# A memory-augmented recurrent attention layer: streamed weights, B-token keys and chain buffers rearranged

## The chip, the cores and the metric

The kernel runs on one core of one Trainium2 chip. The metric is the device time of one execution in microseconds (us); of several runs the median is taken. The engines are called as the profile calls them: PE (matmul), PEld (its weight load), ACT (scalar), DVE (vector), POOL (GpSimd), SP (SyncE, which here only issues transfers).

## What is computed

The model applies four layers to x of shape [1, 2048, 640]: A, B, A, B, each behind a layer norm and with a residual sum. Only A matters here. It cuts the 2048 rows into 64 segments of 32 and carries a memory of 8 rows from each segment to the next:

```python
# A, per segment s: xs = 32 normalised rows, mem = 8 rows
h = concatenate([mem, xs])                                   # L = 40 rows of 640
q, k, v = (einsum('td,dhe->hte', h, w) for w in (Wq, Wk, Wv))  # 32 heads of 192
mask = (idx[:, None] < M) | (idx[:, None] >= idx[None, :])   # M = 8
p = softmax(where(mask, einsum('hqe,hke->hqk', q, k) * 192 ** -0.5, -1e9))
o = einsum('hte,hed->td', einsum('hqk,hke->hqe', p, v), Wo)
mem = o[:8]                                                  # for the next segment
out[s] = o[8:]
```

The chain over segments is serial: the next segment's q, k and v of the memory rows need the memory rows of this one. Wq, Wk, Wv and Wo have 640 x 6144 elements each, in bf16 (6144 = 32 heads of 192). Layer B is a linear attention over all rows without such a chain.

## The kernel before

**Split of the tokens.** The last 8 of a segment's 40 tokens (the "B tokens") have K, Q and V that come from x alone, and their outputs do not enter the memory, so layer A runs in three parts. `A_pre` (L297 to L361) computes K, Q and V of the B tokens of all segments in large matmuls and stores them to DRAM (`kqb_d`, L350; `vb_d`, L361). `A_chain` (L363) walks the 64 segments with the 32 other tokens (8 of memory, 24 of x). `A_post` (L499) multiplies the B tokens' attention outputs with Wo.

**Rounds.** A segment is done in four rounds r of eight heads. In a round, three groups of 20 matmuls (L419, one group for each of K, Q, V) make the projections from hT, the transposed 32 tokens, and five k-blocks b of weights; the four PE row/column groups g of 32 work side by side. ACT evacuates K and Q to `raw` (L427), DVE transposes `raw` into QT (L429) and KT (L434 to L436); ACT and DVE copy V into Vp (L422, L424). The B tokens' Q is copied into QT by POOL (L409). Scores go into one PSUM bank: a mask by a matmul with an identity (L440), the keys of the 32 tokens (L445) and the keys of the B tokens (L449, 8 columns of kqb a head). ACT takes the exponent E (L453), PE sums it with a block of ones (L454, L456), ACT makes the reciprocal by lns and rc (L459, L461), DVE multiplies (Pt, L463 and L465). The values give O (L470; the B tokens' from vb, 8 rows, L474), which ACT and DVE copy into OT (L479, L480); POOL copies the B tokens' columns into otb (L481), and 48 matmuls add the round into W (L484).

**End of a segment.** DVE transposes the next rows (Hx) into hT (L383), transposes W into wt (L491), adds the residual Xr into ob (L494) and copies the new memory into hT (L492), with which the next segment begins. POOL stores otb (L487) and the four pieces of ob (L496).

**Weights.** A weight matrix is cut into 20 pieces (4 rounds, 5 k-blocks) of 128 x 1536 elements, 384 KB; there are 60 for K, Q and V. 36 stay in SBUF (b of 0 to 2, names wK, wQ, wV), 24 are streamed again in every segment: `pieces` (L284) loads b = 3 and 4 of one matrix and round together, 768 KB with rows of 6 KB, into a ring of three buffers called `wring` (L286), from copies that the kernel made at its start. That is 9.44 MB a segment. wo_res, all of Wo, is resident too.

**Order.** The program is written as loops, and a scheduler orders each engine's instructions; buffer counts of the pools decide how far ahead a load or a copy can go. SP issues the weights' ring, Xr (L377 to L379, from x or the residual) and Hx; POOL issues kqb (two a segment, L401), vb (eight a segment, L404), otb and ob. Xr, Hx, KT and Vp have two named buffers each; QT, E, lns, rc, Pt, OT, ob, kqb and vb two each from the pool.

Of the kernel before, what the change touches and what calls it, by code (L numbers as in the profile page):

```python
# [8 lines left out]
P = 128  # L9
BF16 = mybir.dt.bfloat16  # L10
# [5 lines left out]
MASK_NEG = -30000.0  # L16
LN_EPS = 1e-5
# [81 lines left out]
class Kernel:  # L99
# [73 lines left out]
    def build_B_consts(self, dram):  # L173
# [6 lines left out]
        with tc.tile_pool(name="bconst_tmp", bufs=1) as tp:  # L180
# [4 lines left out]
            dq = RR([nc.sync, nc.gpsimd])  # L185
# [14 lines left out]
    def layernorm(self, x_dram, xn_dram, li):  # L200
# [3 lines left out]
        with tc.tile_pool(name=f"ln{li}", bufs=3) as lp:  # L204
            dq = RR([nc.sync, nc.gpsimd])
# [24 lines left out]
    def build_A_consts(self):  # L230
# [3 lines left out]
        mk = const.tile([P, 112], BF16, name="mask_st")  # L234
        nc.gpsimd.memset(mk[:], 0.0)
        for e in range(2):
            m = mk[0:32, 40 * e + 16:40 * e + 40]
            nc.gpsimd.affine_select(out=m, in_=m, compare_op=ALU.is_ge, fill=MASK_NEG, base=8, pattern=[[1, 24]],
                                    channel_multiplier=-1)
            m = mk[0:32, 80 + 16 * e:80 + 16 * e + 8]  # L240
            nc.gpsimd.affine_select(out=m, in_=m, compare_op=ALU.is_ge, fill=MASK_NEG, base=0, pattern=[[1, 8]],
                                    channel_multiplier=-1)
            m = mk[0:32, 80 + 16 * e + 8:80 + 16 * e + 16]
            nc.gpsimd.affine_select(out=m, in_=m, compare_op=ALU.is_ge, fill=MASK_NEG, base=7, pattern=[[0, 8]],
                                    channel_multiplier=-1)
# [10 lines left out]
        for r in range(4):  # L256
            for m in "KQV":
                t = self.dram.tile([P, 2, 1536], BF16, name=f"wst{m}{r}")
                nc.sync.dma_start(out=t[:], in_=self.wview[m][:, 3:5, 1536 * r:1536 * r + 1536])
                self.wst[m, r] = t  # L260

    def layer_A(self, x_dram, xn_dram, xout_dram, li):
# [3 lines left out]
        NR = 4  # L266
        PW = 1536
        self.kqb_d = dram.tile([NSEG, P, NR, 224], BF16, name=f"kqb{li}")
        self.vb_d = dram.tile([NSEG * 8, NR, 4, 512], BF16, name=f"vb{li}")
        self.otb_d = dram.tile([NSEG, P, 384], BF16, name=f"otb{li}")  # L270
        wview = self.wview
        streamed = {(m, r, b) for m in "KQV" for r in range(NR) for b in (3, 4)}
        with tc.tile_pool(name=f"A{li}_wres", bufs=1) as wres:
# [10 lines left out]
            def pieces(pool, m, r, nb=3):  # L284
                t = pool.tile([P, 2, PW], BF16, name="wring", tag="wring", bufs=nb)
                nc.sync.dma_start(out=t[:], in_=self.wst[m, r][:])  # L286
                out = [res[m, r, b][:, :] for b in range(3)] + [t[:, 0, :], t[:, 1, :]]
                return out

            self.A_pre(xn_dram, li, pieces)  # L290
            for r in range(NR):
                nc.sync.dma_start(out=wo[:, 12 * r:12 * r + 12, :], in_=self.A_Wo.rearrange("h d m -> (h d) m").rearrange(
                    "(c p) m -> p c m", p=P)[:, 12 * r:12 * r + 12, :])
            self.A_chain(x_dram, xn_dram, xout_dram, li, pieces, wo)
            self.A_post(x_dram, xout_dram, li, wo)

    def A_pre(self, xn_dram, li, pieces):  # L297
# [4 lines left out]
        with tc.tile_pool(name=f"A{li}_pre", bufs=1) as pp, \  # L302
                tc.tile_pool(name=f"A{li}_preps", bufs=8, space=bass.MemoryType.PSUM) as ps_:
            xv = xn_dram.rearrange("(s t) d -> t s d", t=32)
            xBT = pp.tile([P, KC, 8 * NSEG], BF16, name="xBT")
            for k in range(NT):
                xb = pp.tile([P, 640], BF16, name="xB", tag="xB", bufs=1)
                for t2 in range(TP):
                    nc.gpsimd.dma_start(out=xb[NSEG * t2:NSEG * t2 + NSEG, :], in_=xv[24 + TP * k + t2])
# [4 lines left out]
                for t2 in range(TP):  # L314
                    t = TP * k + t2
                    ev.copy(out=xBT[:, :, :].rearrange("p b (s t) -> p b s t", t=8)[:, :, :, t],
                            in_=pt[:, 0:640].rearrange("p (b q) -> p b q", b=KC)[:, :, NSEG * t2:NSEG * t2 + NSEG])
            stage = [pp.tile([P, 16, 224], BF16, name=f"stage{i}") for i in range(2)]
            vst = [pp.tile([P, 4, 512], BF16, name=f"vst{i}") for i in range(1)]
            for t in stage:  # L320
                nc.vector.memset(t[:], 0.0)
            for t in vst:
                nc.vector.memset(t[:], 0.0)
# [410 lines left out]
```

## Time and profile before

| what | value |
|---|---|
| four runs | 5946.53, 5938.78, 5925.62, 5921.52 us, median 5932.2 |
| the profiled execution's own time | 5946.53 us |
| its span in the profile | 5944.4 us (2.1 us lie around it) |
| granted PE clock, mean | 0.877 |
| bytes moved | 1479 MB, mean 249 GB/s |
| ring loads | 1560 of 768 KB |
| chain, layer 1 | about 373 to 2540 us of the span |
| chain, layer 2 | about 3284 to 5500 us |
| A_pre of layer 1 | matmuls from 156 to 358 us |

How to read the profile: each engine has a share of busy time; 40 slices give busy tenths over the span and the bytes that the DMA engines moved. The chain that ended last follows the work back from the last instruction, so its shares say on what the end depended. A row of the timeline has start, length, engine, line, operation, result and operands, and how many were merged. Groups and waits name who ended an idle time; "issue" is time in which an engine waited for nothing that the profile shows. SPq, ACTq and POOLq are the engines' own issuing of transfers.

### The profile page before, as it was taken

To read this page: it belongs to the slowest core of one execution; us is meant where nothing else is said; L and a number is where in the kernel's file an instruction comes from. 1 tells how busy PE (TensorE), PEld (TensorE's weight loads), DVE (VectorE), ACT (ScalarE), POOL (GpSimd) and SP (SyncE) were. 2 spreads that over 40 slices of the span, in tenths; PEclk is the share of its full clock that TensorE was granted. 3 is DMA by queue.
4 is the path that set the end of the run, shared out by engine and by line. 5 is a ranking of instruction groups with operands and counts; after the bars stand their busy time and mean duration, and the time that the engine had idled before them with its cause. 6 is when DMAs were issued, how large, how long until landed. Compare 5 with 4: busy or idle time off the path is not lost.

```text
span 5944.4 us, 224613 instructions
## 1 busy us (share of the span) xinstructions
PE 4271.4 (72%) x99784; PEld 2569.8 (43%) x99784; DVE 2232.8 (38%) x6994; ACT 1587.3 (27%) x4729; POOL 1530.7 (26%) x3332
## 2 busy tenths in 40 slices
PE   0877777777777777757858677777777777777778
PEld 0744444444444444434337344444444444444343
DVE  2333333333333333337454333333333333332383
ACT  0322222222222222223123222222222222222230
POOL 3122233233333323220011332233333222332100
PEclk9988888888888988879879888888898888888888
DMA  5668888888888888840066788888888888887201
GB/s 186 234 223 295 299 297 306 286 305 301 301 304 297 306 297 296 295 136 1 21 222 209 270 300 299 297 299 303 294 311 303 289 292 287 298 309 240 92 22 32
DMA packets 423998, 1479.35 MB, mean 249 GB/s; under 512 B 119392, under 2 KB 175680, under 8 KB 423024
## 3 DMA queue, kind: packets, MB, share of 16 engines
q1 hardware_dynamic: 330000, 1329.03, 62.6%
q0 software_dynamic: 91648, 135.06, 7.2%
q8 instruction: 780, 12.78, 0.8%
q14 instruction: 194, 1.59, 0.1%
q10 hardware_dynamic: 1376, 0.88, 0.1%
HBM read 1382.25 MB, written 91.79 MB: 248 GB/s over the span
## 4 chain that ended last, share of the span: by engine, by line
PE 41%; DMA 28%; issue 11%; DVE 9%; ACT 8%; POOL 1%; SPq 1%; DVEq 0%; ACTq 0%; POOLq 0%
PE ps_qkv L419 17%; DMA wring<-wstV 12%; DMA wring<-wstQ 10%; PE ps_w L484 7%; DMA wring<-wstK 3%; ACT raw L427 2%; DVE QT L429 2%; PE ps_num L542 2%; PE ps_s L445 2%; ACT Vp L422 2%; PE ps_kv L542 2%; PE ps_bqk L542 1%; PE pp L519 1%; PE ps_o L470 1%; ACT OT L479 1%
## 5 line engine op out<-in xcount | busy, mean ns | idle before, releaser
L419 PEld LDWEIGHTS <-hT 128*32 128x32 bf16 x30720 | 930.4, 104 | 1121.2 <-issue 775.5
L419 PE MATMUL ps_qkv<-wring,hT 128*32 128x384 bf16 x12288 | 1020.8, 362 | 227.9 <-DMA wring<-wstQ 85.3
L427 ACT ACTIVATE raw<-ps_qkv 128x384 bf16<-128x384 f32 x1024 | 502.9, 491 | 1611.6 <-PE ps_qkv L419 1571.1
L484 PE MATMUL ps_w<-wo_res,OT 128*32 128x160 bf16 x24576 | 658.7, 262 | 163.8 <-ACT OT L479 76.6
L419 PE MATMUL ps_qkv<-wK,hT 128*32 128x384 bf16 x6144 | 567.4, 382 | 211.8 <-DVE hT L492 98.5
L404 POOL DMA_DIRECT2D vb<-vb x1024 | 571.2, 559 | 485.7 <-PE ps_o L474 344.8
L419 PE MATMUL ps_qkv<-wQ,hT 128*32 128x384 bf16 x6144 | 656.2, 385 | 34.9 <-issue 21.6
L484 PEld LDWEIGHTS <-OT 128*32 128x32 bf16 x24576 | 519.2, 108 | 326.1 <-ACT OT L479 219.0
L409 POOL COPY QT<-kqb 128x96 bf16<-128x96 bf16 x512 | 136.1, 266 | 1639.7 <-PE ps_s L449 1632.7
L434 DVE STREAM_TRANSPOSE KT<-raw 128x128 bf16<-128x128 bf16 x1024 | 258.6, 291 | 636.9 <-ACT raw L427 629.5
L429 DVE STREAM_TRANSPOSE QT<-raw 128x384 bf16<-128x384 bf16 x512 | 296.2, 578 | 490.3 <-ACT raw L427 487.0
L424 DVE CAST Vp<-ps_qkv 128x192 bf16<-128x192 f32 x512 | 183.3, 358 | 790.0 <-ACT Vp L422 790.0
L419 PE MATMUL ps_qkv<-wV,hT 128*32 128x384 bf16 x6144 | 424.5, 364 | 16.5 <-issue 13.8
L480 DVE CAST OT<-ps_o 128x240 bf16<-128x240 f32 x512 | 208.8, 408 | 506.2 <-ACT OT L479 506.2
L422 ACT ACTIVATE Vp<-ps_qkv 128x192 bf16<-128x192 f32 x512 | 169.5, 331 | 757.9 <-PE ps_s L449 710.6
L445 PE MATMUL ps_s<-QT,KT 128*32 128x40 bf16 x8192 | 220.0, 184 | 159.5 <-DVE QT L429 102.6
L481 POOL COPY otb<-OT 128x96 bf16<-128x96 bf16 x512 | 139.0, 272 | 725.4 <-DVE OT L480 725.4
L479 ACT ACTIVATE OT<-ps_o 128x240 bf16<-128x240 f32 x512 | 190.1, 371 | 492.2 <-PE ps_o L474 492.2
L496 POOL DMA_DIRECT2D xres<-ob x512 | 264.3, 523 | 141.8 <-DMA kqb<-kqb 93.0
L445 PEld LDWEIGHTS <-KT 128*32 128x32 bf16 x8192 | 148.4, 94 | 339.5 <-DVE QT L429 294.5
L470 PE MATMUL ps_o<-Pt,Vp 32*128 32x40 bf16 x8192 | 221.2, 180 | 96.1 <-DVE Pt L463 95.7
L470 PEld LDWEIGHTS <-Vp 32*128 32x128 bf16 x8192 | 195.1, 93 | 213.7 <-issue 204.8
(412 smaller groups left out, 6163.6 us busy)
## 6 DMA issues: line engine op xcount, KB each, us to landing
wring<-wstK SPq DMA_DIRECT2D x520, 768.0 KB
wring<-wstQ SPq DMA_DIRECT2D x520, 768.0 KB
wring<-wstV SPq DMA_DIRECT2D x520, 768.0 KB
kqb<-stage POOLq DMA_DIRECT2D x32, 896.0 KB, 6.4
kqb<-kqb POOLq DMA_DIRECT2D x256, 112.0 KB, 6.4
vb<-vst POOLq DMA_DIRECT2D x32, 512.0 KB, 2.9
vb<-vb POOLq DMA_DIRECT2D x1024, 16.0 KB, 5.6
wo_res<-in_A_Wo_dram SPq DMA_DIRECT2D x8, 1920.0 KB
```

Of the source, the lines that this page charges most:

```text
L404: nc.gpsimd.dma_start(out=vb[32 * g:32 * g + 8, :, :], in_=self.vb_d[8 * s:8 * s + 8, r:r + 2, g, :])
L419: nc.tensor.matmul(ps[32 * g:32 * g + 32, 0:384], lhsT=hT[:, b, :], rhs=rhs, start=(b == 0), stop=(b == KC - 1), tile_position=(0, 32 * g) ...
L422: nc.scalar.activation(out=Vp[:, :].rearrange("p (a c) -> p a c", c=64)[:, 0:3, :], in_=ps[:, 0:192].rearrange("p (a c) -> p a c", c=64), ...
L427: nc.scalar.activation(out=raw[:], in_=ps[:, 0:384], func=ACT.Copy)
L429: nc.vector.transpose(out=QT[:, :, 8:40], in_=raw[:, :].rearrange("p (c j) -> p c j", j=32))
L434: nc.vector.transpose(out=kv[:, :, o, :], in_=rv[:, :, i, :])
L445: nc.tensor.matmul(S[32 * g:32 * g + 32, 40 * e:40 * e + 40], lhsT=KT[:, 4 * g + ks, :], rhs=QT[:, 3 * g + qc, :], start=False, stop=False ...
L470: nc.tensor.matmul(O[:, g, 40 * i:40 * i + 40], lhsT=Vp[32 * g:32 * g + 32, P * blk:P * blk + P], rhs=Pt[32 * g:32 * g + 32, 40 * e:40 * e ...
L479: nc.scalar.activation(out=ov[:, 0:2, :], in_=O[:, 0:2, 0:120], func=ACT.Copy)
L484: nc.tensor.matmul(W[32 * g:32 * g + 32, 0:160], lhsT=OT[:, c, 8:40], rhs=wo[:, 12 * r + c, 160 * g:160 * g + 160], start=(r == 0 and c == 0),
L496: nc.gpsimd.dma_start(out=xout_dram[32 * s:32 * s + 24, 160 * g:160 * g + 160], in_=ob[32 * g + 8:32 * g + 32, :])
L542: nc.tensor.matmul(ps[rows, n0:n0 + nn], lhsT=lhsT_fn(k), rhs=rhs_fn(k, n0, nn), **kw)
```

## The change

- 20 pieces are streamed in place of 24: all twelve of b = 4, the four of V with b = 3 and the four of Q with b = 3. Each is a load of its own (384 KB, rows of 3 KB), and the ring has four such buffers (three in A_pre). In a round that is one piece of K, two of Q and two of V; 40 pieces stay resident, and 7.86 MB a segment are streamed.
- kqb and vb come in one load each a segment, issued by SP, each with one buffer. vb holds the B tokens' values of the four rounds in one block of 32 rows for each g; POOL copies the B tokens' keys once a segment into kb, with the four rounds' keys of a head side by side (32 columns). B scores and B values work on these 32 rows, and a mask for each round shuts out the keys of the other three.
- One buffer in place of two for KT, Vp, Xr, QT, E, lns, rc, Pt, OT, ob, kqb and vb; wt takes a buffer of raw's.
- No transfer is issued by POOL any more: otb and ob are stored by ACT, the norms' and layer B's transfers alternate between SP and ACT.
- A_pre: the B tokens are held by token instead of by segment, so four large copies replace 32 small ones; K and Q have one staging buffer each with a store of its own (rows of 256 and 192 B, in place of 448 B, and two stages used in turn); vb is stored by two transfers a block. The load of wo_res stands ahead of A_pre.
- A_post: two issuing queues, one xrB buffer, and the residual is added in place.

```diff
+STREAM = ([(m, r, 4) for r in range(4) for m in "KQV"] + [(m, r, 3) for m in "VQK" for r in range(4)])
+NSTREAM = 20
...
-            def pieces(pool, m, r, nb=3):
-                t = pool.tile([P, 2, PW], BF16, name="wring", tag="wring", bufs=nb)
-                nc.sync.dma_start(out=t[:], in_=self.wst[m, r][:])
-                out = [res[m, r, b][:, :] for b in range(3)] + [t[:, 0, :], t[:, 1, :]]
+            def pieces(pool, m, r, nb=4):
+                out = []
+                for b in range(KC):
+                    if (m, r, b) in streamed:
+                        t = pool.tile([P, PW], BF16, name="wring", tag="wring", bufs=nb)
+                        nc.sync.dma_start(out=t[:], in_=streamed[m, r, b][:])
+                        out.append(t)
+                    else:
+                        out.append(res[m, r, b])
                 return out
-            self.A_pre(xn_dram, li, pieces)
             for r in range(NR):
                 nc.sync.dma_start(out=wo[:, 12 * r:12 * r + 12, :], in_=self.A_Wo.rearrange("h d m -> (h d) m").rearrange(
                     "(c p) m -> p c m", p=P)[:, 12 * r:12 * r + 12, :])
+            self.A_pre(xn_dram, li, pieces)
...
-                    nc.gpsimd.dma_start(out=xb[NSEG * t2:NSEG * t2 + NSEG, :], in_=xv[24 + TP * k + t2])
+                    nc.scalar.dma_start(out=xb[NSEG * t2:NSEG * t2 + NSEG, :], in_=xv[24 + TP * k + t2])
...
-            stage = [pp.tile([P, 16, 224], BF16, name=f"stage{i}") for i in range(2)]
-            vst = [pp.tile([P, 4, 512], BF16, name=f"vst{i}") for i in range(1)]
+            stk = pp.tile([P, 16, P], BF16, name="stk")
+            stq = pp.tile([P, 16, 96], BF16, name="stq")
+            vt = pp.tile([P, 4, 512], BF16, name="vst")
...
-                    nc.gpsimd.dma_start(out=self.kqb_d[16 * tb:16 * tb + 16, :, r, :].rearrange("s p f -> p s f"), in_=st[:])
+                        c0, c1, st = (0, 128, stk) if m == "K" else (128, 224, stq)
+                        nc.sync.dma_start(out=self.kqb_d[16 * tb:16 * tb + 16, :, r, c0:c1].rearrange("s p f -> p s f"),
+                                          in_=st[:])
...
-            kts = [sp.tile([P, 16, 32], BF16, name=f"KT{i}", bufs=1) for i in range(2)]
-            vps = [sp.tile([P, 512], BF16, name=f"Vp{i}", bufs=1) for i in range(2)]
+            KT = sp.tile([P, 16, 32], BF16, name="KT", bufs=1)
+            Vp = sp.tile([P, 512], BF16, name="Vp", bufs=1)
...
-            xrs = [sp.tile([P, 160], BF16, name=f"Xr{i}", bufs=1) for i in range(2)]
+            xrs = [sp.tile([P, 160], BF16, name="Xr", bufs=1)]
...
-                load_rows(xrs[s % 2], x_dram, s)
+                load_rows(xrs[0], x_dram, s)
...
+                kqb = sp.tile([P, NR, 224], BF16, name="kqb", tag="kqb", bufs=1)
+                nc.sync.dma_start(out=kqb[:], in_=self.kqb_d[s])
+                vb = sp.tile([P, 512], BF16, name="vb", tag="vb", bufs=1)
+                nc.sync.dma_start(out=vb[:], in_=self.vb_d[s].rearrange("g r j c -> (g r j) c"))
+                kb = sp.tile([P, 16, NR, 8], BF16, name="kb", tag="kb", bufs=1)
+                nc.gpsimd.tensor_copy(out=kb[:, :, :, :], in_=kqb[:, :, 0:128].rearrange("p r (c t) -> p c r t", t=8))
...
-                                nc.tensor.matmul(S[32 * g:32 * g + 8, 80 + 16 * e:96 + 16 * e], lhsT=kb[:, 4 * g + ks, :],
+                                nc.tensor.matmul(S[32 * g:32 * g + 32, 80 + 16 * e:96 + 16 * e],
+                                                 lhsT=kb[:, 4 * g + ks, :, :].rearrange("p r t -> p (r t)"),
...
-                    QT = sp.tile([P, 12, 40], BF16, name="QT", tag="QT")
+                    QT = sp.tile([P, 12, 40], BF16, name="QT", tag="QT", bufs=1)
...
-                nc.gpsimd.dma_start(out=self.otb_d[s], in_=otb[:, :, :, :].rearrange("p r c t -> p (r c t)"))
+                nc.scalar.dma_start(out=self.otb_d[s], in_=otb[:, :, :, :].rearrange("p r c t -> p (r c t)"))
...
-                ob = sp.tile([P, 160], BF16, name="ob", tag="ob")
-                nc.vector.tensor_tensor(out=ob[:], in0=W[:, 0:160], in1=xrs[s % 2][:], op=ALU.add)
+                ob = sp.tile([P, 160], BF16, name="ob", tag="ob", bufs=1)
+                nc.vector.tensor_tensor(out=ob[:], in0=W[:, 0:160], in1=xrs[0][:], op=ALU.add)
                 for g in range(4):
-                    nc.gpsimd.dma_start(out=xout_dram[32 * s:32 * s + 24, 160 * g:160 * g + 160],
+                    nc.scalar.dma_start(out=xout_dram[32 * s:32 * s + 24, 160 * g:160 * g + 160],
                                         in_=ob[32 * g + 8:32 * g + 32, :])
```

## The prediction

> **What bounds the kernel now.** I read the page's busy shares first, then the slices, then the chain of work that ended last.
>
> ```profile
> PE 4271.4 (72%) x99784; PEld 2569.8 (43%) x99784; DVE 2232.8 (38%) x6994; ACT 1587.3 (27%) x4729; POOL 1530.7 (26%) x3332
> ...
> DMA  5668888888888888840066788888888888887201
> GB/s 186 234 223 295 299 297 306 286 305 301 301 304 297 306 297 296 295 136 1 21 222 209 270 300 299 297 299 303 294 311 303 289 292 287 298 309 240 92 22 32
> ...
> PE 41%; DMA 28%; issue 11%; DVE 9%; ACT 8%; POOL 1%; SPq 1%; DVEq 0%; ACTq 0%; POOLq 0%
> PE ps_qkv L419 17%; DMA wring<-wstV 12%; DMA wring<-wstQ 10%; PE ps_w L484 7%; DMA wring<-wstK 3%; ACT raw L427 2%; DVE QT L429 2%; PE ps_num L542 2%; PE ps_s L445 2%; ACT Vp L422 2%; PE ps_kv L542 2%; PE ps_bqk L542 1%; PE pp L519 1%; PE ps_o L470 1%; ACT OT L479 1%
> ```
>
> The DMA row shows two plateaus near 300 GB/s: the two chains of 64 segments (about 373 to 2540 us and 3284 to 5500 us), some 4320 of the 5944 us. A quarter of the ending chain is the streamed weights on their way (12+10+3%). No engine is full; the path goes round between PE, ACT, DVE and the ring.
>
> One boundary between segments shows how. SyncE's own row first (start, length, line, transfer, count), then the chain of waits there:
>
> ```profile
> 1543.10 0.32 SPq L286 DMA_DIRECT2D wring<-wstQ  x1
> 1545.00 0.32 SPq L286 DMA_DIRECT2D wring<-wstV  x1
> 1545.37 1.64 SPq L379 DMA_DIRECT2D Xr<-in_A_x_dram  x4
> 1547.05 4.56 SPq L379 DMA_DIRECT2D Hx<-xn  x4
> 1551.71 0.34 SPq L286 DMA_DIRECT2D wring<-wstK  x1
> ```
> ```profile
> 1529.50 6.36 DMA wring<-wstV
> ...
> 1543.10 6.22 DMA wring<-wstQ
> ```
>
> A 768 KB piece needs over 6 us from issue to use, and for the 6.4 us from 1545.3 to 1551.7 SyncE asks for no weights. Windows of that time: 341 GB/s at 0.95 DMA share in 1523 to 1549, then 56 GB/s in 1549.5 to 1553. So inside the rounds the transfers are the limit, and at each boundary they pause.
>
> Between the arrivals of hT (DVE at L492), 61 segments of layer 1 take 33.77 us in the mean. Cut at the four Pt (L463) they are: hT to Pt0 7.11; rounds 1 to 3 7.65, 8.22 and 7.07; Pt3 to hT 3.72. The shortest rounds take 6.14, rounds in which the ring was on time.
>
> **The change, part by part.**
>
> *Fewer streamed bytes.* 24 pieces of 384 KB become 20: 9.44 MB a segment become 7.86. The rest is kqb 0.23, vb 0.13 (0.13 before), otb 0.10, and Xr, Hx and xout 0.09, so 8.4 MB. At the 341 GB/s of the saturated window this is 24.7 us a segment, under the 33.77. Transfers no longer fill the rounds. What is late next is the dependent chain itself: QKV matmuls, raw, transposes, scores, E, lns, rc, Pt, O, OT, W. Its row is the shortest round, 6.14. To it I add the fetch stalls: in the waits of PE from 450 to 2400 us (57 segments) the "issue" entries sum to about 85 us, 1.5 a segment, 0.36 a round. So 6.5 a round with the ring on time.
>
> *Ring of four single pieces.* The ring holds 1.5 MB in place of 2.25, and a round takes five pieces, so each is asked for after four fifths of a round. Unloaded, a 768 KB piece went from issue 373.43 to use 378.03: 4.6 us. Resident loads with the same 3 KB rows ran at about 390 GB/s (132 to 164 us), so half the bytes take 1.0 us less: 3.5 us. Four pieces back in time, with gaps of 1 to 2 us between matmul groups, leaves 4.1 to 5.1 of the 6.14 us, which covers 3.5, and does not always cover a loaded 4.5 (three pieces queued at about 1 us each). Cost 0 to 1 us a round; I take 0.5, nearer to the unloaded row as the load falls. Rounds: 7.0.
>
> *Order on SyncE at the boundary.* In the changed program's order the next K04, Q03, Q04 and V03 are issued before the segment ends, where now K waits for eight row loads (1551.71). Then come vb, Hx x4, Xr x4, and only behind those V04 and round 1. As Xr has a single buffer, its first load waits for the previous ob (L494), just after the segment's end. Queued behind it are V04 and K14 to V14; PE's O(0) waits for V04. By the rows: ob ends about 0.3 us after W, four Xr issues take 1.64, V04 has its 3.5: about 6 us after hT, where O(0) is wanted at 7.1. If the waits for earlier transfers stretch these issues as they did the four Hx (4.56), it is 2 us late. Cost 0 to 2 us, taken 0.1: part one 7.2.
>
> *Issues from POOL to ACT and SP.* POOL loses 2x0.57 + 8x0.56 + 0.59 + 4x0.52 = 8.3 us a segment, and is 1% of the chain: nothing gained, though its own wait row (POOL L404 idle for ps_o) goes too. ACT gains the otb store and four xout stores. ACT issues in A_post took 1.82 us for five (0.36 each). They stand ahead of raw K of the new segment, which moves from 1.3 us after hT to between 1.9 and 2.7. Raw Q comes only 3.9 after hT, so after K's transposes (0.51+0.26+0.31) and QT (0.58) scores start at 4.9, against 5.0 now. Taken 0.1 at the tail: 3.8. Without that cover it is up to 1.4.
>
> *Single KT, Vp, QT, E, lns, rc, Pt, OT.* PE's order already puts the reader ahead of the next writer: KT of round r+1 is written after scores(r), Vp after O(r). Nothing; if V copies were to wait for O(r), up to 0.36 a round (the longer Vp copy).
>
> *Shared 32-row blocks.* Matmul counts and streamed columns stay: B scores write 32 rows in place of 8, B values read 32 in place of 8. The new POOL copy of 512 elements: between the 96-element copy (0.27) and five of them (1.45); it lies in POOL's idle time, before scores(0). Nothing, up to 1.45 if kqb comes late.
>
> Sum of a segment: 7.2 + 3x7.0 + 3.8 = 32.0 us, 1.77 less; 128 segments give -226 us. Bounds: 7.1 + 3x6.5 + 3.7 = 30.3 (-444) and 35 (rival B).
>
> *A_pre.* The two stages become one K and one Q stage. Now a pair (r, tb) takes 6.9 us, evacuation-bound (K 4.0, Q 2.6). The store row is:
>
> ```profile
> kqb<-stage POOLq DMA_DIRECT2D x32, 896.0 KB, 6.4
> ```
>
> Its 2048 packets stay 2048 for K and 2048 for Q. If packets set its price, a store still takes 6.4 us, if bytes, 4.7; I take 5.6. K's copies (4.0) then wait for K's store: 9.6 a pair, 2.7 more, 16 pairs and the four V parts with similar waits: +35 a layer, between 0 (stores beside the other stage's copies) and 60. xB loads leave POOL (7.3 us a block of four): -7. So +28 a layer, +56 in all.
>
> The Trainium skill ("DMA: Bandwidth & Descriptors", Specifications) says that descriptors under 512 B miss the line rate, since the DMA must read, modify and write; that speaks against rows of 256 and 192 B. The trace already shows 448 B rows landing in 6.4 us where 512 KB in 4 KB rows take 2.9; by the rule both new stores would keep the full packet price, and the pair would be 10.4 us.
>
> *A_post.* Now 14.6 us a block, 13 of it PE. With stores on ACT ahead of its otw copies (1.48 each) and a single xr: +2 a block, +8 a layer, +16 (0 to 50). *Start-up:* 20 copies of 384 KB for 9.44 MB: -4. Layer B and the norms: same transfers on other queues, 0 +- 10.
>
> Sum: -226 + 56 + 16 - 4 = -158. The profiled execution took 5946.5 (span 5944.4 and 2.1 around it): 5788. It is the slowest of the four runs, 14 above their median 5932.2, so the forecast against the median is about 5775.
>
> **Rivals.**
> A, *the whole saving arrives*: the ring is always on time, 30.3 us a segment: 5932 - 444 + 68 = 5556. For it: 24.7 us of transfer leaves slack, and the prefetch over the boundary. Against: ring of four, 1 to 2 us gaps.
> B, *the boundary queue eats it*: SyncE's Xr loads wait for ob, and V04 and round 1 behind them start so late that O(0) and round 1 are 2 us late; with a loaded piece at 4.5 us each later round adds 1. Then 9.2 + 3x7.5 + 3.8 = 35.5 at worst, likelier 34.5: 5932 + 0.73x128 + 68 = 6093. It decides slower from 33.2 us a segment on (33.77 less 68/128). For it: DMA idles now just where Xr and Hx are issued, and these loads stretch. Against: four of round 0's five pieces are there by then.
> C, *no gain*: transfers were hidden by the dependent chain, segments stay at 33.2: 5932 +- 18. For it: ring waits on PE are only 87.5 us in 57 segments. Against: the ending chain gives DMA 28%.
>
> **How the numbers follow.** A measurement of this kernel can tell about 0.3% (18 us). Chances: forecast (5690 to 5870) 0.42, A 0.18, C 0.15, B 0.25. C is split: 0.09 in the band, 0.04 under it, 0.02 above. Faster: 0.42 + 0.18 + 0.04 = 0.64; same 0.09; slower 0.25 + 0.02 = 0.27. The range reaches most of A and B: 5570 to 6090; the forecast's own is 5690 to 5870.
>
> **What would show it.** Right: a segment near 32.0 with rounds near 7.0; DMA share in the chain about 0.75 in place of 0.84; ring entries in PE's waits below 1.5 us a segment. Wrong: SyncE idle before Xr for ob and V04 issued 3 us or more after hT with O(0) waiting for wring (B); rounds under 6.6 (A); A_pre outside 200 to 260 us from first matmul to the chain (now 202, forecast 230), or ACT's raw K more than 3 us after hT.

## The result, and the profile after

The changed kernel takes 5949.7 us in the median of 49 runs (5919.8 to 5980.1), the kernel before 5928.1 us in the median of 75 (5906.3 to 5960.9). The ratio is 1.0034, 95% interval 1.0025 to 1.0042: slower by a third of a per cent, where 5775 us and a clear gain had been forecast.

One caution on reading the two traces: the profiled execution of the kernel before took 5946.5 us, 18 above its median, that of the changed kernel 5926.9, 23 below its own. So the traces flatter the change by 41 us, or 0.3 us in each of 128 segments.

From the page of the changed kernel, the rows that answer to those shown of before (busy shares; DMA share and bytes by slice; the chain that ended last, by engine and by line):

```profile
PE 4203.6 (71%) x99784; PEld 2462.3 (42%) x99784; DVE 2211.4 (37%) x6982; ACT 1588.2 (27%) x4725; POOL 355.9 (6%) x1199
...
DMA  4767777777777777750066677777777777776301
GB/s 155 226 168 249 262 257 261 251 256 249 257 258 256 256 253 252 263 158 1 21 220 163 200 263 253 262 252 260 251 263 254 257 256 256 256 257 223 104 22 33
...
DMA 49%; PE 28%; DVE 10%; ACT 6%; issue 4%; SPq 3%; ACTq 1%; POOL 0%; DVEq 0%; POOLq 0%
DMA wring<-wstV 24%; PE ps_qkv L422 12%; DMA wring<-wstK 8%; DMA wring<-wstQ 2%; PE ps_w L487 2%; PE ps_num L544 2%; DMA otb<-otb 2%; PE ps_bqk L544 2%; PE ps_kv L544 1%; DMA Hx<-xn 1%; DMA vb<-vb 1%; ACT E L456 1%; DMA kqb<-stq 1%; PE ps_o L473 1%; DMA vb<-vst 1%
```

The bytes fell as planned, from some 300 to 256 GB/s on the plateaus. But the share of the ending chain that is a transfer rose from 28 to 49%, and "issue" fell from 11 to 4%. Fewer bytes move, and the path waits for them longer.

PE's waits in 450 to 2400 us (waiting line, releaser: total us, times, longest) show the same exchange. The changed kernel first:

```profile
PE ps_qkv L422 <- DMA wring<-wstV: 131.1, 184, 2.3
...
PE ps_qkv L422 <- DMA wring<-wstQ: 40.9, 65, 1.2
...
PE ps_qkv L422 <- DMA wring<-wstK: 34.8, 54, 2.5
...
PE ps_qkv L422 <- issue: 10.3, 11, 1.4
...
PE ps_w L487 <- issue: 7.4, 10, 1.4
```

and the kernel before, in its own trace:

```profile
PE ps_qkv L419 <- DMA wring<-wstQ: 36.4, 68, 1.3
...
PE ps_qkv L419 <- DMA wring<-wstK: 31.0, 48, 1.4
PE ps_w L484 <- issue: 29.8, 34, 2.2
PE ps_qkv L419 <- issue: 23.6, 27, 2.7
PE ps_qkv L419 <- DMA wring<-wstV: 20.1, 39, 1.6
```

Summed over all lines, waits for the ring went from 87.5 to 206.8 us, and "issue" from 85.4 to 18.4. "issue" is called a fetch stall from here on: that PE waits there for its instructions is shown below, with the ring's depth. One wait took the other's place.

By stage, in us (mean of the segments between two arrivals of hT, cut at the Pt of each round; layer 1; layer 2 is within 0.4):

| kernel | segment | hT to Pt0 | round 1 | round 2 | round 3 | Pt3 to hT |
|---|---|---|---|---|---|---|
| before | 33.76 | 7.11 | 7.64 | 8.24 | 7.06 | 3.72 |
| changed | 33.25 | 6.76 | 8.47 | 6.84 | 7.49 | 3.69 |

The 62 segments between the first and the last hT became shorter by 32 us together in layer 1 and by 45 us in layer 2. Against that, the first hT comes 37.5 us later (447.7 against 410.2), the time from the last hT of layer 1 to the first of layer 2 grew by 32.5 us, and what follows the last hT shrank by 12.4. Together that is -19 us in the traces, which the caution above turns into +22, as measured.

Round 1 got longer. At the end of a segment SyncE does this in the changed kernel (start, length, line, transfer, count):

```profile
1509.76 0.32 SPq L295 DMA_DIRECT2D wring<-wstV  x1
1512.12 0.32 SPq L407 DMA_DIRECT2D vb<-vb  x1
1512.49 1.61 SPq L387 DMA_DIRECT2D Hx<-xn  x4
1515.18 2.16 SPq L387 DMA_DIRECT2D Xr<-in_A_x_dram  x4
1517.44 0.35 SPq L295 DMA_DIRECT2D wring<-wstV  x1
1518.41 0.34 SPq L295 DMA_DIRECT2D wring<-wstK  x1
```

hT is there at 1515.25. vb had waited for the last O of the segment, Xr for ob; no weights are asked for from 1510.1 to 1517.4, and the K piece of round 1 is issued at 1518.4. Over 450 to 2400 us this pause has a median of 8.1 us, and the piece behind it (V04, the V piece with b = 4 of round 0) is issued 3.2 us after hT in the median. Behind the boundary the chain of waits goes from one piece to the next:

```profile
1518.41 4.70 DMA wring<-wstK
...
1523.55 4.79 DMA wring<-wstV
...
1530.22 5.13 DMA wring<-wstV
```

A piece of half the size takes 4.7 to 5.1 us from issue to use in these rows, not half of the 6.2 to 6.4 of before. Of the 197 pieces on this chain in 450 to 2400 us the median is 4.7 us, with nine tenths between 3.0 and 6.2; before, 90 pieces of 768 KB had a median of 6.6. And most pieces are issued only when a buffer comes free: 684 of the 1174 loads there waited on SyncE for PE to use one.

### The profile page after: what moved, and what is told of

It is laid out like the page before. It is cut to its first block, busy times and chain, and to the rows that moved or that the text cites. A ratio compares the mean times of both kernels' runs of the same rounds, so it can differ in the third digit from the quotient of the medians.

```text
span 5925.1 us, 226967 instructions
## 1 busy us (share of the span) xinstructions
PE 4203.6 (71%) x99784; PEld 2462.3 (42%) x99784; DVE 2211.4 (37%) x6982; ACT 1588.2 (27%) x4725; POOL 355.9 (6%) x1199
## 3 DMA queue, kind: packets, MB, share of 16 engines
q8 instruction: 779, 12.76, 0.9%
## 4 chain that ended last, share of the span: by engine, by line
DMA 49%; PE 28%; DVE 10%; ACT 6%; issue 4%; SPq 3%; ACTq 1%; POOL 0%; DVEq 0%; POOLq 0%
DMA wring<-wstV 24%; PE ps_qkv L422 12%; DMA wring<-wstK 8%; DMA wring<-wstQ 2%; PE ps_w L487 2%; PE ps_num L544 2%; DMA otb<-otb 2%; PE ps_bqk L544 2%; PE ps_kv L544 1%; DMA Hx<-xn 1%; DMA vb<-vb 1%; ACT E L456 1%; DMA kqb<-stq 1%; PE ps_o L473 1%; DMA vb<-vst 1%
## 5 line engine op out<-in xcount | busy, mean ns | idle before, releaser
L422 PEld LDWEIGHTS <-hT 128*32 128x32 bf16 x30720 | 864.2, 106 | 1346.9 <-issue 1014.1
L422 PE MATMUL ps_qkv<-wK,hT 128*32 128x384 bf16 x8192 | 718.3, 389 | 136.0 <-DVE hT L495 113.5
L487 PEld LDWEIGHTS <-OT 128*32 128x32 bf16 x24576 | 486.4, 106 | 426.6 <-ACT OT L482 273.3
L422 PE MATMUL ps_qkv<-wQ,hT 128*32 128x384 bf16 x6144 | 569.0, 392 | 10.4 <-issue 10.2
L466 DVE TENSOR_TENSOR Pt<-E,rc 128x80 bf16<-128x80 bf16 x512 | 124.3, 243 | 542.7 <-ACT rc L464 542.1
L473 PEld LDWEIGHTS <-Vp 32*128 32x128 bf16 x8192 | 179.3, 93 | 247.7 <-issue 148.1
L447 PEld LDWEIGHTS <-KT 128*32 128x32 bf16 x8192 | 174.4, 95 | 149.6 <-DVE QT L432 130.3
L451 PE MATMUL ps_s<-QT,kb 128*32 128x16 bf16 x8192 | 215.3, 172 | 0.9 <-issue 0.9
## 6 DMA issues: line engine op xcount, KB each, us to landing
kqb<-kqb SPq DMA_DIRECT2D x128, 224.0 KB
```

The costliest lines, as they stand in the source:

```text
L422: nc.tensor.matmul(ps[32 * g:32 * g + 32, 0:384], lhsT=hT[:, b, :], rhs=rhs, start=(b == 0), stop=(b == KC - 1), tile_position=(0, 32 * g) ...
L447: nc.tensor.matmul(S[32 * g:32 * g + 32, 40 * e:40 * e + 40], lhsT=KT[:, 4 * g + ks, :], rhs=QT[:, 3 * g + qc, :], start=False, stop=False ...
L451: nc.tensor.matmul(S[32 * g:32 * g + 32, 80 + 16 * e:96 + 16 * e], lhsT=kb[:, 4 * g + ks, :, :].rearrange("p r t -> p (r t)"), rhs=QT[:, 3 ...
L473: nc.tensor.matmul(O[:, g, 40 * i:40 * i + 40], lhsT=Vp[32 * g:32 * g + 32, P * blk:P * blk + P], rhs=Pt[32 * g:32 * g + 32, 40 * e:40 * e ...
L487: nc.tensor.matmul(W[32 * g:32 * g + 32, 0:160], lhsT=OT[:, c, 8:40], rhs=wo[:, 12 * r + c, 160 * g:160 * g + 160], start=(r == 0 and c == 0),
```

## Experiments

The theories were D (the ring of four single pieces is too shallow, so each round waits for issue to use), T (the bytes themselves are the limit, 3 KB rows being dearer), B (SyncE's order at the end of a segment takes the gain), and later F (weights and instruction fetch share the transfers, so that depth exchanges one wait for the other). Ratios are to the kernel before, run beside it on the same chip, with their 95% intervals. The rows other than the change's come from four chips, on which the kernel before took 5915 to 5926 us, so a difference of some 10 us between rows of different chips says nothing.

| run | pieces, ring | other edits | median us | ratio to before |
|---|---|---|---|---|
| e5_ring3_of20 | 20, 3 | | 6419.4 | 1.083 (1.081 to 1.085) |
| the change | 20, 4 | | 5949.7 | 1.003 (1.003 to 1.004) |
| f3_ring6_of20 | 20, 6 | two pieces left out | 5782.7 | 0.977 (0.974 to 0.980) |
| e1_ring6_of22 | 22, 6 | | 5886.3 | 0.994 (0.992 to 0.996) |
| e2_ring8_of24 | 24, 8 | | 6317.3 | 1.067 (1.065 to 1.069) |
| e4_xr2_vb2 | 20, 4 | two Xr, two vb | 5904.2 | 0.997 (0.996 to 0.999) |
| e9_boundary_20_4 | 20, 4 | relieved | 5851.7 | 0.989 (0.986 to 0.993) |
| f1_boundary_20_6 | 20, 6 | relieved, two pieces left out | 5712.3 | 0.966 (0.963 to 0.969) |
| e7_ring6_rows_pool | 22, 6 | rows on POOL | 5763.5 | 0.972 (0.970 to 0.974) |
| e10_boundary_22_6 | 22, 6 | relieved | 5754.6 | 0.971 (0.969 to 0.974) |
| f2_boundary_24_6 | 24, 6 | relieved | 5885.7 | 0.995 (0.993 to 0.997) |
| e11_boundary_24_8 | 24, 8 | relieved | 5840.7 | 0.986 (0.984 to 0.989) |

"Relieved" means: Xr and Hx issued by POOL, two buffers for Xr and for vb. The deeper rings are paid for with resident pieces: 22 and 24 pieces use the SBUF of the two or four given up. All kernels with 22 or 24 pieces also have a ring of four, in place of three, in A_pre.

### No weights streamed in the chain (e3_chain_resident)

```diff
-                    if (m, r, b) in streamed:
+                    if (m, r, b) in streamed and nb == 0:
+                        out.append(res[m, r, 0])
+                    elif (m, r, b) in streamed:
...
-                        w = pieces(sp, m, r)
+                        w = pieces(sp, m, r, 0)
```

> Changed kernel whose chain reads the resident piece b = 0 wherever it would read a streamed one (so the projections are not the reference's), with no ring in the chain; A_pre still streams. It gives the price of all ring waits. D and T: a segment falls to about 28 to 30 us, 5400 to 5500 us in all. B: the waits at the boundary stay (vb, Hx, otb stores: some 2 us a segment), a segment of about 31.

Measured: 5264.6 us in one run, under the 5400 to 5500 expected by D and T; a segment of 28.1 us in the mean (6.48, then 5.87, 6.19, 6.16, and 3.39), as D and T had it, and not B's 31. So the attention chain alone is 28 us long, stores on ACT ahead of raw K and the single buffers included, and streaming cost the changed kernel 5.1 us a segment. 3.8 of these are PE's two waits above; what makes the other 1.3 is not separated. The forecast's rival C, that transfers are hidden by that chain, is out, although its time (33.2 us a segment, no gain) is the one that came.

In this run no wait for the ring can be left in PE's list, but there is no "issue" in its chain either. The same instructions were fetched, and the page shows the instruction queue's bytes (name, kind: packets, MB, share):

```profile
q8 instruction: 780, 12.78, 1.0%
```

as against 779 packets and 12.76 MB in the changed kernel. In these runs fetching costs PE time only where weights are streamed beside it.

### The ring's depth at equal bytes (e5, f3, f1)

Each is the changed kernel with one number, `nb=4`, made 3 or 6. For six, SBUF is made by leaving two resident pieces out:

```diff
+                            if m == "K" and r >= 2 and b == 3:
+                                res[m, r, b] = res[m, r, 2]
+                                continue
...
-            def pieces(pool, m, r, nb=4):
+            def pieces(pool, m, r, nb=6):
```

> Changed kernel with a ring of three in place of four, the same 20 pieces. Theory D (depth): waits of PE for the ring rise above the 207 us that 57 segments of the changed kernel show, a segment 34.5 or more, 6100 us or more. Theory F (weights and instruction fetch share the transfers, so that depth trades one wait for the other): the ring waits rise as well, the fetch stalls fall from 18 us to under 10; 6050 or more. Theory T (bytes alone): as many bytes, unchanged, 5930 to 5970.

> The changed kernel with a ring of six in place of four (the same two resident pieces left out and read from another one), everything else as in the change, SyncE's order at the boundary too. It tells what the change would have given if the ring had stayed deep: D alone says a segment of 32.0 or less, 5780 or less; B says the boundary then holds it at 32.5 to 33, 5830 to 5900.

> The relieved kernel with 20 pieces and a ring of six: two of the resident K pieces (b = 3 of rounds 2 and 3) are left out of SBUF and the piece b = 2 is read in their place, so the projections of K there are not the reference's; bytes streamed as in the change. Depth at equal bytes, against the relieved 20 with a ring of four (5852 us): D says ring waits fall from 224 us to about 60 in 57 segments and the time to 5650 to 5700; F says that the fetch stalls rise from 21 to 80 or more us, and the time only falls to 5700 to 5760; T says no change.

Measured: 6419.4 with three, 5949.7 with four, 5782.7 with six, at the same bytes in the chain. T, the bytes alone, falls. With six the segment is 32.1 us, and the time 8 us from the forecast's 5775 (some 20 by the ratio); D alone had allowed 32.0 and 5780 or less, B 5830 to 5900. Some 11 us of the difference to the trace with four lie outside the chains. With the boundary relieved as well (f1), 5712.3 lies in F's range and above D's 5650 to 5700. PE's waits of the kernel with six (f3) in the same 1950 us:

```profile
PE ps_qkv L425 <- issue: 37.3, 40, 2.5
PE ps_w L490 <- issue: 36.5, 32, 2.7
PE ps_s L450 <- issue: 34.7, 23, 2.9
PE ps_qkv L425 <- DMA wring<-wstV: 22.4, 36, 1.7
PE ps_s L454 <- issue: 21.7, 15, 2.2
```

Only 22.4 us of ring waits are left of 206.8, but 140.8 of fetch stalls stand where 18.4 were. That is F.

That these stalls are waits for instructions can be read from the packets of the instruction queue, which the trace holds one by one. There are 780 of 16 KB for 2 x 99784 matmuls and weight loads of PE, one for every 256. One stall of the kernel with six (start, length, engine, line, operation, result and operands, count, idle time before and its end):

```profile
1263.95 0.22 PE L450 MATMUL ps_s<-QT,KT 128*32 128x40 bf16 x3 [2.60 <-issue]
```

PE stood from 1261.35; a packet of the instruction queue ran from 1261.33 to 1262.38, and PE went on 1.6 us after it. So it is with all 126 stalls of this kernel, the 92 of the kernel before and the 22 of the changed one: each ends 1.2 to 1.6 us after such a packet has landed. The packet itself takes 0.96 to 1.03 us in the median in every kernel of the table below. What differs is when it starts. The last column counts PE's instructions run when the n-th packet starts, less 256 n (median): the higher, the later PE's next instructions are on their way.

The sums of both waits, 450 to 2400 us of each trace, and that count (with nothing streamed to 2150 us, as its chain ends earlier):

| kernel | ring waits, us | fetch stalls, us | start of a fetch, PE instructions |
|---|---|---|---|
| nothing streamed | 0 | 0 | 227 |
| 20, ring 3 | 285.2 | 2.6 | 247 |
| 20, ring 4 (the change) | 206.8 | 18.4 | 284 |
| 20, ring 4, relieved | 224.0 | 20.8 | 285 |
| 20, ring 6 | 22.4 | 140.8 | 333 |
| 20, ring 6, relieved | 17.7 | 152.1 | 320 |
| 22, ring 6 | 78.9 | 77.1 | 297 |
| 22, ring 6, relieved | 68.7 | 137.3 | 329 |
| 24, ring 6, relieved | 98.1 | 169.2 | 333 |
| 24, ring 8 | 146.3 | 78.1 | 297 |
| 24, ring 8, relieved | 55.7 | 168.2 | 343 |
| before (24 in pairs, ring 3 pairs) | 87.5 | 85.4 | 321 |
| before, loaded singly, ring 6 (e6) | 40.9 | 118.8 | 317 |

With three or four pieces at once the stalls are under 0.5 us a segment; with six or more they are 1.3 to 2.9. The two lowest of these, 77.1 and 78.1 us, are the kernels with 22 and 24 pieces whose boundary is not relieved, so depth alone does not set the price. That fetches start later where more pieces are under way is shown; that they stand in line behind the weights' own packets is the likely reason, and was not tried by itself.

The Trainium skill ("Runtime: NRT & Kernel Launch", Instruction fetch mechanics) says that each sequencer fetches 16 KiB blocks by a DMA queue of its own and that the cost is mostly hidden. The first half goes with the queue's row above (12.78 MB in 780 packets are 16 KB each); of the second the runs show that it holds with no weights or few under way (0 to 21 us in 1950), and not with a ring of six (141 us with 20 pieces).

### The end of a segment (e4, e7, e9, e10)

```diff
-            xrs = [sp.tile([P, 160], BF16, name="Xr", bufs=1)]
+            xrs = [sp.tile([P, 160], BF16, name=f"Xr{i}", bufs=1) for i in range(2)]
...
-                vb = sp.tile([P, 512], BF16, name="vb", tag="vb", bufs=1)
+                vb = sp.tile([P, 512], BF16, name="vb", tag="vb", bufs=2)
...
-                    nc.sync.dma_start(out=dst[32 * g + 8:32 * g + 32, :], in_=src[32 * s:32 * s + 24, 160 * g:160 * g + 160])
+                    nc.gpsimd.dma_start(out=dst[32 * g + 8:32 * g + 32, :], in_=src[32 * s:32 * s + 24, 160 * g:160 * g + 160])
```

e4 has the two buffers only, e7 the rows on POOL only (with 22 pieces, ring of six), e9 and e10 both.

> Changed kernel with two buffers for Xr and for vb, as before the change; all else unchanged. Theory B: SyncE no longer waits for the last O of a segment before vb, Hx and the next pieces; a segment loses 1 to 2 us, 5700 to 5830 us. D and T: the ring decides, less than 0.5 us a segment, 5890 to 5950 us.

> The variant with 22 pieces and a ring of six, with the row loads Xr and Hx issued by POOL, so that SyncE goes on with weights at the end of a segment; Xr still has one buffer. Theory B (what is lost at the boundary is SyncE's order): the time from hT to the second Pt falls from 16.3 us to about 14, a segment to 31, 5650 to 5750 us. Without B (the transfers are busy all the same): 5860 to 5900, and fetch stalls rise.

> Changed kernel (20 pieces, ring of four) with the end of a segment relieved: Xr and Hx issued by POOL, two buffers for Xr and for vb, so SyncE is never behind ob or the last O with its weights. Theory B (order at the boundary takes the gain): 1.5 to 2 us a segment less than the changed kernel, 5690 to 5760 us. Theory D (ring depth): rounds 2 and 3 stay at 6.8 and 7.4, and the gain is under 0.8 us a segment, 5840 to 5900.

> The same relief with 22 pieces and a ring of six. B and D together: some 0.5 us a segment under the run with only the row loads on POOL (5763 us), 5680 to 5730. If only fetch and transfers are left (F): equal to it, 5745 to 5780, with more fetch stalls.

Measured: the buffers give 45 us (5949.7 to 5904.2, as D had it), the rows on POOL another 53 (to 5851.7): 98 us, 0.8 a segment, just what D had allowed and half of what B had asked for. Rounds 2 and 3 stay at 6.7 and 7.4, as D had said. In the kernel with 22 pieces and six buffers the rows alone give 123 us (5886.3 to 5763.5, a little above B's 5750), and the time from hT to the second Pt falls from 16.4 to 14.0 us as foreseen, though rounds 2 and 3 give 1.2 back: a segment of 32.3, not 31. The two buffers add 9 us there, within the noise; 5754.6 is F's number, but the fetch stalls did not rise with it (141.9 to 137.3). So the order at the boundary is a cause, and the second one: 98 us at the ring of four and 70 at six (5782.7 to 5712.3), against 140 to 167 us for the depth. By the ratios these are 85, 69 and 139 to 155. With 22 pieces the boundary is worth 132 us.

How the 0.8 us arise is open. The pause between two weight loads at the end of a segment hardly shrinks: its median is 7.3 us in the relieved kernel (e9), 8.1 in the changed one. One boundary of e9, where hT is there at 1490.2:

```profile
1484.56 0.32 SPq L295 DMA_DIRECT2D wring<-wstV  x1
1487.12 0.32 SPq L407 DMA_DIRECT2D vb<-vb  x1
1492.13 0.32 SPq L295 DMA_DIRECT2D wring<-wstV  x1
```

With nothing else to issue but vb, SyncE still waits 7.6 us: the four buffers are full, and the first comes free only when PE has hT and uses a piece. V04 is now issued 1.9 us after hT in every segment in place of 3.2 in the median, but PE's ring waits did not fall (206.8 to 224.0).

### Bytes at equal depth, and the form of a load (e1, e2, e11, f2, e6)

e1 and e2 change `NSTREAM` and `nb` (and give A_pre a ring of four); e11 and f2 do so with the boundary relieved. e6 is the kernel before with its 24 pieces loaded singly:

```diff
-                t = pool.tile([P, 2, PW], BF16, name="wring", tag="wring", bufs=nb)
-                nc.sync.dma_start(out=t[:], in_=self.wst[m, r][:])
-                out = [res[m, r, b][:, :] for b in range(3)] + [t[:, 0, :], t[:, 1, :]]
+                out = [res[m, r, b][:, :] for b in range(3)]
+                for b in (3, 4):
+                    t = pool.tile([P, PW], BF16, name="wring", tag="wring", bufs=2 * nb)
+                    nc.sync.dma_start(out=t[:], in_=self.wst[m, r, b][:])
+                    out.append(t[:, :])
```

> Changed kernel with 22 pieces streamed (two more of K, b = 3) and a ring of six. Theory D (the ring is too shallow: with four single pieces the path is the time from a freed buffer to the next use, 4.9 us in the median): in spite of 0.79 MB more a segment it is faster than the changed kernel, a segment about 32 us in place of 33.2, so about 5800 us. Theory T (the transfers themselves are the limit, 3 KB rows being dearer for each byte): 10% more pieces cost up to 10% of the ring's time, a segment 34 to 35, 6050 to 6150 us. Theory B (the order at the boundary between segments): unchanged within 0.5%.

> Changed kernel with 24 pieces streamed and a ring of eight, the same SBUF again. D alone: the ring waits go under 50 us in 57 segments, a segment under 32.5, below 5850 us. F: the ring waits go under 60, but the fetch stalls rise above 90 us; a segment 33.0 to 33.5, 5880 to 5930. T: 20% more bytes, slower than the changed kernel by 2% or more.

> The same relief with 24 pieces and a ring of eight. If it was SyncE's vb and Xr waits that made the variant of 24 and eight slow (6317 us), it falls to 5700 to 5800; if the bytes made it slow, it stays above 6100. Between the three relieved kernels: D says more depth is faster, T says fewer bytes are faster, and F that they differ by under 1%.

> The relieved kernel with 24 pieces and a ring of six: more bytes at equal depth, against 22 with six (5755 us). T and F: 5820 to 5900, the bytes cost what they take. D: as six buffers now hold one round of six pieces, like the ring of the kernel before, no more than 30 us slower.

> Kernel before with the same 24 streamed pieces, each loaded by itself (384 KB, 3 KB rows) into a ring of six, so the same bytes in SBUF and on the way; only the form of the load changes. T: 3 KB rows are dearer, 2 to 5% slower (6050 to 6200 us). D: as many bytes ahead and freed earlier, so the same within 1% or a little faster (5870 to 5950 us). B says nothing on it: same.

Measured: with six buffers and the boundary relieved, 20, 22 and 24 pieces take 5712, 5755 and 5886 us. Four pieces fewer are worth 174 us, three quarters of the forecast's 226, as long as the ring stays at six (A_pre has three buffers with 20 pieces and four with the others, and the 20 leave two pieces out). f2 lies where T and F had it; D, at most 30 us slower than 22 pieces, missed by 101. So depth is not all: bytes cost too. e1 gains 63 us over the change although it streams 10% more. That has D's sign, but a segment of 33.1 us and not D's 32; neither T's 6050 to 6150 nor B's unchanged time came. e6 is no slower than the kernel before, 5902.6, ratio 0.997 (0.995 to 0.998), so 3 KB rows are not dear: the form of the load is cleared. There too the ring waits fell (87.5 to 40.9) and the fetch stalls rose (85.4 to 118.8).

e2 went against D by 470 us and against F by 390; T's "slower by 2% or more" is what came. Its SyncE row points elsewhere: the vb load, with one buffer, waits for the last O of the segment, and behind it stand the next segment's weights (waiting line, releaser: total us, times, longest):

```profile
SPq L407 <- PE ps_o L477: 297.8, 53, 7.7
```

With rows, Xr and vb relieved (e11) the same 24 of eight take 5840.7, 477 us less at the same bytes and 45 less than 24 of six: above the 5700 to 5800 expected, but far from the 6100 that the bytes would have kept. The three reliefs came together, so vb's part is not separated. With 24 pieces a ring of eight only helped once the engine that issues it was free to fill it.

### ACT's stores and A_pre (e12, f4, e8)

e12 is e10 with the stores of otb and ob on POOL (`nc.scalar` to `nc.gpsimd` in two lines), f4 is e12 with the load of wo_res behind A_pre, e8 is e2 with two K and two Q stages used in turn.

> The relieved kernel with 22 pieces and a ring of six, with the stores of otb and ob issued by POOL in place of ACT, as before the change. If ACT's four stores ahead of raw K hold up a segment's start: 0.3 to 0.8 us a segment less, 40 to 100 us under the same kernel with stores on ACT. If raw K has slack, as the prediction had it: within 15 us of it.

> The fastest kernel so far (22 pieces, ring of six, rows and stores on POOL, two Xr and vb; 5727 us) with the load of wo_res behind A_pre again, as before the change. If the first stores of A_pre wait behind the 7.9 MB of wo_res: 15 to 20 us a layer less, 5690 to 5700. If the load only moves its cost to the start of the chain: 5715 to 5740.

> The variant with 24 pieces and a ring of eight, with two K stages and two Q stages in A_pre. Against that variant: if the stores of the single stages hold A_pre up, the time before each chain falls by 20 to 35 us, 40 to 70 us in all; if not, nothing.

Measured: e12 5727.3 us (0.967, 0.965 to 0.970), 27 less than e10, between the two expectations: raw K had slack, but not all. f4 5708.0 (0.964, 0.962 to 0.967), 19 less than e12, between its two expectations; it is the fastest of the kernels that compute all, 242 us under the change. e8 6302.7 (1.064, 1.062 to 1.065), only 15 less than e2, where 40 to 70 were asked for. From the first matmul of A_pre to the chain of layer 1 the traces have these times in us, cut at the first V matmul of round 0:

| kernel | to the first V matmul | from there to the chain | together |
|---|---|---|---|
| before | 29.2 | 187.8 | 217.0 |
| changed | 66.7 | 188.6 | 255.3 |
| e2 (24, ring 8) | 63.7 | 175.4 | 239.1 |
| e8 (e2 with two stages) | 56.9 | 169.7 | 226.6 |
| e12 (22, ring 6) | 63.1 | 171.3 | 234.4 |
| f4 (e12, wo_res behind) | 48.2 | 180.2 | 228.4 |

All of the 38 us is lost in round 0, where the first K store waits on SyncE's queue until 189 us, behind the last weights and the four loads of wo_res:

```profile
172.91 15.95 SPq L302 DMA_DIRECT2D wo_res<-in_A_Wo_dram  x4
188.96 5.15 SPq L357 DMA_DIRECT2D kqb<-stk  x1
```

Moving wo_res back gives 15 us there and takes 9 again behind it. What else keeps round 0 at 48 us was not tried by itself, nor was the ring of four that e2, e12 and f4 have in A_pre.

## Why the prediction was wrong

**The step that failed is the sizing of the ring of four.** The prediction put it at "0 to 1 us a round; I take 0.5", from an unloaded piece of 3.5 us. Loaded pieces took 4.7 us in the median on the chain of waits, and PE's ring waits are 3.5 us a segment (206.8 in 58.6 segments) where three rounds of 0.5 had been taken. "Does not always cover a loaded 4.5" was in the text, as a bound; it was the rule. Half of these waits, 1.8 us, are for the last piece of rounds 1 to 3, the V piece with b = 4. At six buffers and the same bytes the time is 5783 us, close to the forecast, but in part by luck: the ring costs 0.4 us a segment there and the fetch 2.3, where 1.5 and 1.1 had been taken for the three rounds.

By stage, in us (the waits are PE's, from the changed kernel's trace, layer 1):

| | hT to Pt0 | round 1 | round 2 | round 3 | Pt3 to hT | sum |
|---|---|---|---|---|---|---|
| forecast | 7.2 | 7.0 | 7.0 | 7.0 | 3.8 | 32.0 |
| measured | 6.76 | 8.47 | 6.84 | 7.49 | 3.69 | 33.25 |
| ring waits in it | 0.04 | 1.54 | 0.86 | 1.10 | 0 | 3.5 |
| fetch stalls in it | 0 | 0.12 | 0.04 | 0.15 | 0.01 | 0.3 |

The three rounds took 1.8 us more than forecast: the ring 2.0 more, the fetch 0.8 less, and 0.6 that neither list names. The two ends of a segment took 0.55 less.

**The second term was the boundary on SyncE**, taken at 0.1 us with a bound of 2. Relieving it was worth 0.8 us a segment, though not by the path that the text named: PE waits only 0.14 us a segment for V04. The loss stands in round 1 (7.64 before, 8.47 changed), which the relief alone brings to 7.5 and the deeper ring alone to 6.9. The pause in the weights there, 8.1 us, is for the most part the full ring again: 7.3 remain with the row loads moved to POOL and two buffers for Xr and vb.

**The fetch stalls were taken as a constant** (0.36 a round on top of 6.14). They are not: 0 without streaming, 0.3 us a segment at a ring of four, 2.3 to 2.5 at six with the same pieces. This error went the other way and made up a part of the first.

**Right:** the chain alone (rounds of 6.14; the run without streaming has 5.87 to 6.19, with the single buffers and the shared 32-row blocks in it, which were not tried by themselves), the DMA share in the chain (0.77 against 0.75 foreseen), and the size of a store: on the chain of waits a K or Q store after round 0 takes 3.9 to 6.5 us, 5.6 had been taken. The issues moved from POOL to ACT, taken at 0.1 us a segment, were worth 0.2 where they were moved back (27 us, e12). That saturated transfers limited the kernel before is likely, but no run takes the streaming out of that kernel.

**Right only in its sum** is what lies outside the segments: 37.5 us to the first hT, 32.5 between the layers and -12.4 at the end make 58 where 68 were forecast. A_pre itself lost 38 us in layer 1 where 28 were forecast, and elsewhere than foreseen: pairs of round 1 come every 7.6 us (K stores at 245.1, 252.9, 260.5 and 267.8), not 9.6, since the stores lie beside the other stage's copies, and the loss is round 0's instead. (The B tokens' copies in A_pre were eight of 1.57 us before, not 32.) The Trainium skill's rule on descriptors under 512 B, weighed there, would have given 10.4 us a pair; the measurement is under both.

**Slips in its sums** that decide little: 4.6 less 1.0 is 3.6, not 3.5; a K store priced by bytes is 6.4 x 512/896 = 3.7 us, and the 4.7 follows from no row; 16 pairs of 2.7 us are already 43, more than the 35 taken.

**The rivals.** B named the mechanisms (the boundary and loaded pieces) and set their price too high: 34.5 us a segment, 33.2 came. Its sign, V04 3 us or more after hT, holds in 33 of 58 segments; its O(0) waiting for it does not. C named the time, 33.2 us a segment, with a mechanism that the run without streaming refutes, and not even by that mechanism: segments left as they were would have stayed at 33.77.

## What to carry to other kernels

Saving streamed bytes and shrinking the ring that carries them are two changes: before giving up buffers, set the time of a loaded piece from issue to use against the time in which its buffer comes round again. Keep the queue that fills a ring free of any load with a single buffer: in these kernels everything behind such a load waited for that buffer's last reader. And where "issue" stalls fall while waits for transfers rise, add both up before calling either a gain.

## What the hardware showed unexpectedly

Fetch stalls depend on what else is on the way: 2.6, 18.4 and 140.8 us in 1950 us with three, four and six pieces in the ring, and none with nothing streamed, at nearly the same number of fetched bytes. A fetch takes the same 0.96 to 0.98 us in these four; it starts later.

The three slowest kernels (20 with a ring of three, 24 with a ring of eight, the latter also with two stages) had the lowest mean clock, 0.82 to 0.83 against 0.85 or more in all others. The trace of the variant with 24 pieces and a ring of eight shows it in one segment (window: length, five engines' busy times with counts, granted clock, DMA share, GB/s):

```profile
1483.00:1488.00 5.00, 3.49 (x151) 2.51 (x145) 2.74 (x10) 1.89 (x6) 0.88 (x2) 1.00 0.53 168
1488.00:1494.00 6.00, 4.68 (x111) 2.96 (x96) 1.09 (x5) 0.37 (x1) 0.48 (x2) 0.50 0.56 180
1494.00:1500.00 6.00, 3.06 (x71) 1.41 (x63) 1.57 (x5) 1.14 (x3) 0.08 (x1) 0.78 0.76 246
```

The 0.50 at the boundary is nothing special to this kernel: in the first 2 us after hT the mean clock is 0.50 to 0.54 in all seven kernels read for it (this one and its relieved form, before, changed, 20 pieces with three and with six buffers, nothing streamed). Special is a second drop. PE waits for the ring here:

```profile
1497.43 0.35 PE L422 MATMUL ps_qkv<-wring,hT 128*32 128x384 bf16 x4 [2.03 <-DMA wring<-wstQ]
```

and from 1498.2 to 1501.6 the clock is 0.50 again. Over 450 to 2400 us the mean clock 8 to 10 us after hT is 0.53 in this kernel and 0.86 with 20 pieces and a ring of three, against 0.98 or more in the other five. So the two of the seven with the longest segments also have more slow matmuls in them; that the waits bring the clock down was not tried.

How much of the 370 us over the changed kernel is due to it was not separated.
